# The k'v products of a head pair as two 64-column halves of the array, in a kernel of linear attention, a cosine feed-forward layer and a soft mixture of experts

## The chip, the cores and the metric

The kernel runs on one core of a Trainium2 chip. The metric is the device time of one execution in microseconds; the time before is the median of three runs. One execution was also taken by the hardware profiler, and all rows shown here are from that one.

## What is computed

All inputs are fp32. First, linear attention over 8 batches of 8 heads with 576 tokens of 64 values; then a feed-forward layer on the 4608 tokens; then a soft mixture of 8 experts with 4 slots each.

```python
kv = np.einsum('bhsd,bhse->bhde', k, v)
out = np.einsum('bhsd,bhde->bhse', q, kv)
rms = np.sqrt(np.mean(out * out, axis=-1, keepdims=True) + 1e-06)
x = (out / rms * g_norm)            # laid out as 4608 x 512
h = x @ w_in                        # 512 -> 2048
x = (h * np.cos(h)) @ w_out         # 2048 -> 512
logits = x @ phi                    # 32 slots
```

The mixture takes a softmax over the tokens of each slot, two expert layers with relu, and a softmax over the slots of each token. The change touches the first line alone: for each batch and head, `kv` is a 64x64 matrix, summed over 576 tokens.

## The kernel before, in words

The tokens are worked on in 12 blocks of 384 (`NB`, index `j`). Of each two batches, two blocks hold the first 384 tokens of one batch each, and the third holds the last 192 of both (`spans`). Each block runs 16 steps (`f`), one per 128 columns of `w_in`. A step is `main` (line 368; its 12 products are at line 375), then the cosine on ScalarE and VectorE (`fr_tt`, `round_off`, `cos_b`, `cos_c`, lines 386 to 416), with other work of PE put between the main products: transposes of the attention output (`att_xT`, line 233), logits (lines 458 and 467), the slot sums (`slot_acc`, line 533), the attention outputs (`att_out`, line 201) and the k'v products (`kv_pair`, lines 178 to 190).

The order is fixed by hand. `PLAN["start"]` lists the tokens of the start one by one, `PLAN["one"]` and `PLAN["two"]` the order within a step of the first two blocks, and the other entries of `PLAN` say in which step of which block each piece of side work runs. The four pairs of batch 0 are the tokens `kv.1 kv.2 kv.0 kv.3` of the start; those of batch 1 stand in the first step, those of batches 2 and 3 in blocks 1 to 3 (`PLAN["K"]`), and those of batch b from 4 on at steps 14, 17, 18 and 19 of a block (`PLAN["kv"]`). PE carries its instructions out in this order; the other engines and SP, which issues all the loads, have orders of their own that follow from the same lists.

`load_kv` (line 161) loads k and v of one batch and one pair of heads: 128 tokens in the partitions, four groups of them, 128 columns for the two heads of the pair. There are four such buffers. The remaining 64 tokens of two batches share one tile (`load_rem`, line 166); `kz` holds k of these with the other batch's 64 rows at zero.

`kv_pair` makes one 128x128 product per group, k as weights and v moving, all five summed in one PSUM tile: four at line 182, the one of the remainder at line 184. Its diagonal 64x64 blocks are k'v of the two heads; the other two blocks would be k of one head with v of the other and are not read. The two copies (`copy_on`, line 140: on ScalarE for batch 0, on VectorE for all others) put the diagonal blocks into `kvbd`, a 128x128 tile per pair with zeros elsewhere, from which `att_out` makes the attention output of both heads at once. `at_bank` (line 136) hands out the four PSUM banks that this side work shares; `main` has three of its own.

In `att_out`, a block of one batch takes 128 tokens as weights; the third block of each two batches takes 64 tokens of each batch as weights, and writes the two products into partitions 0 to 63 and 64 to 127 of the result.

A row gives a product's form as rows x columns of the weights: `128*128` uses all the array, `128*64` one half of its columns, `128*32` a quarter, `64*128` one half of its rows. Behind it stands the size of the moving operand.

Of the kernel before, what the change touches and what calls it, by code (L numbers as in the profile page):

```python
# [40 lines left out]
    stop=None,  # L41
    start=(
# [4 lines left out]
    ),  # L47
# [28 lines left out]
def tile_linear_attention__ffn_cos__soft_moe(  # L76
# [14 lines left out]
    nc = tc.nc  # L91
# [44 lines left out]
    def at_bank(name):  # L136
        return ps_a.tile([128, 512], F32, tag="at", name=name)

    def copy_on(e, out, in_):
        (nc.vector.tensor_copy if e else nc.scalar.copy)(out=out, in_=in_)  # L140


    q_t, kv_t, vr_t = {}, {}, {}
    kz = rem_p.tile([128, 2, 512], F32, tag="kr", name="kz")
# [31 lines left out]


    def kv_pair(b, pr):
        ps = at_bank("kvps")[:, 0:128]
        t = kv_t.pop((b, pr))  # L180
        for r in range(4):
            nc.tensor.matmul(out=ps, lhsT=t[:, 0, r, :], rhs=t[:, 1, r, :], start=(r == 0), stop=False)  # L182
        cc = slice(pr * 128, pr * 128 + 128)
        nc.tensor.matmul(out=ps, lhsT=kz[:, b % 2, cc], rhs=vr_t[b // 2][:, cc], start=False, stop=True)  # L184
        t = kvbd[b % 2]
        e = PLAN["ke"][b] if b < 2 else 2
        copy_on(e, t[0:64, pr, 0:64], ps[0:64, 0:64])
        copy_on(e, t[64:128, pr, 64:128], ps[64:128, 64:128])

        kv_done.add((b, pr))  # L190

# [642 lines left out]
    for b in range(1, B):  # L834
        p, i = divmod(b, 2)
        n, sl = 3 * p - 2 + i, PLAN["kv"]
        if b < 4:
            n, sl = PLAN["K"][b - 1]
        for pr in range(4):
            at2(n, sl[pr], kv_pair, b, pr)  # L840
# [96 lines left out]
    def token(t, f):  # L937
        k, *arg = t.split(".")
        if k.upper() in steps:
            out = int(k.islower())  # L940
            w = int(arg[0]) if arg else f + (PLAN["LO"] if out else PLAN["LI"])
            if w < NF and (arg or w >= (PLAN["PO"] if out else PLAN["PI"])):
                ck(k.upper(), w, out)
                steps[k.upper()](w, out)
        elif arg:
            a = int(arg[0])
            dict(kv=lambda: kv_pair(0, a), ao=lambda: att_out(0, a), xs=lambda: att_xs(0, a),
                 xT=lambda: att_xT(0, a), lo=lambda: att_lo(0, a), warm=lambda: warm(a),
                 win=lambda: load_win(a), wout=lambda: load_wout(a), lkv=lambda: load_kv(a // 4, a % 4),
                 rem=lambda: load_rem(a) if a == 0 else load_kz(0, 1), q=lambda: load_q(a))[k]()  # L950
        else:
            j = int(k[1])
            f -= L * j
            if 0 <= f < NF:
                dict(m=main, s=lambda j, f: run(side, j, f), f=fr_tt, r=round_off, p=lambda j, f: run(post, j, f),
                     b=cos_b, c=cos_c, e=lambda j, f: run(fin, j, f), l=lambda j, f: run(loads, j, f))[k[0]](j, f)
# [103 lines left out]
```

## Time and profile before

| what | us |
|---|---|
| median of 3 runs | 719.67 |
| lowest and highest run | 717.18, 719.83 |
| the profiled execution: its own time | 720.89 |
| its span, from first to last instruction | 719.0 |
| TensorE (PE) busy in the span | 689.0 |
| TensorE loading weights (PEld) | 574.3 |
| VectorE (DVE) busy | 527.1 |
| ScalarE (ACT) busy | 443.8 |
| GpSimd (POOL) busy | 106.5 |

The time of an execution is a little longer than the span of its instructions. Weight loads run beside the products, so the shares of PE and PEld aren't added. A product's busy time contains its way through the array, which overlaps with the next product; what a product costs in a stream is the distance between starts, not its duration. A core's granted clock of TensorE is given as a share of its full speed, 1.00 at most.

### The profile page before, as it was taken

The numbers are of one execution on the slowest core, as the hardware profiler recorded it, in microseconds if no ns is written. First come the engines' busy times: TensorE is split into PE (matmuls) and PEld (weight loads), VectorE is DVE, ScalarE is ACT, GpSimd is POOL, SyncE is SP. The second block draws the span as 40 slices with busy tenths as digits, with TensorE's granted clock in tenths as the row PEclk, the third lists the DMA queues.
The fourth block names the chain that finished last, engine by engine and source line by source line (L and its number), as shares of the span: only waits on it lengthen the run. The fifth ranks groups of instructions, "written<-read, shape, count | busy, mean of one in ns | idle before, by whom it ended". The sixth has DMA issues, their size and how long they took to land.

```text
span 719.0 us, 13016 instructions
## 1 busy us (share of the span) xinstructions
PE 689.0 (96%) x4780; PEld 574.3 (80%) x4780; DVE 527.1 (73%) x1101; ACT 443.8 (62%) x929; POOL 106.5 (15%) x104
## 2 busy tenths in 40 slices
PE   7879999999999999999999999999999999999984
PEld 7768998886998987998898879889979797864353
DVE  2998998477888878788888887888887874345144
ACT  2567997675666676575576756656757557551143
POOL 2342333100302111112012011110120210000400
PEclk9998999999999999999999999999999999999997
DMA  9953452022742674564525745735249278989997
GB/s 323 377 190 138 176 188 78 4 80 100 210 122 67 183 206 124 169 179 103 147 77 148 205 146 154 213 84 152 73 117 305 51 242 269 348 321 347 356 370 320
DMA packets 73886, 134.09 MB, mean 186 GB/s; under 512 B 8416, under 2 KB 50016, under 8 KB 73056
## 3 DMA queue, kind: packets, MB, share of 16 engines
q1 hardware_dynamic: 73824, 133.27, 58.7%
q8 instruction: 38, 0.62, 0.3%
q14 instruction: 24, 0.20, 0.1%
HBM read 91.29 MB, written 13.63 MB: 146 GB/s over the span
## 4 chain that ended last, share of the span: by engine, by line
PE 82%; DVE 9%; ACT 4%; issue 2%; DMA 1%; SPq 0%; POOL 0%; DVEq 0%; ACTq 0%
PE h L375 50%; PE ab L533 5%; PE kvps L182 4%; PE l L458 4%; PE ops L201 4%; PE xTps L233 2%; PE tr L431 2%; PE eo L689 2%; PE eh L663 2%; DVE gT L410 1%; DVE tt L396 1%; PE l L467 1%; PE fo L714 1%; PE kvps L184 1%; DVE tr L416 1%
## 5 line engine op out<-in xcount | busy, mean ns | idle before, releaser
L375 PE MATMUL h<-xt,w 128*128 128x384 f32 x2304 | 438.0, 342 | 1.6 <-DVE xt L246 1.2
L375 PEld LDWEIGHTS h<-xt,w 128*128 128x128 f32 x2304 | 397.2, 189 | 29.1 <-DVE gT L410 8.9
L401 ACT ACTIVATE fr<-tt 128x384 f32<-128x384 f32 x192 | 100.4, 524 | 136.5 <-DVE tt L396 136.0
L410 DVE TENSOR_TENSOR gT<-fr,h 128x384 f32<-128x384 f32 x186 | 102.8, 553 | 58.6 <-ACT fr L401 58.4
L213 POOL TENSOR_TENSOR ri<-ss,mhalf 128x8 f32<-128x8 f32 x36 | 65.5, 1825 | 430.8 <-DVE ss L211 430.8
L396 DVE SCALAR_TENSOR_TENSOR tt<-tt,fr 128x384 f32<-128x384 f32 x192 | 106.5, 559 | 28.9 <-ACT tt L391 27.5
L391 ACT ACTIVATE tt<-fr 128x384 f32<-128x384 f32 x192 | 100.9, 525 | 6.1
L389 ACT ACTIVATE fr<-h 128x384 f32<-128x384 f32 x192 | 92.7, 483 | 18.2 <-PE h L375 18.0
L416 DVE STREAM_TRANSPOSE tr<-gT 128x384 f32<-128x384 f32 x144 | 83.3, 579 | 5.1 <-DVE gT L410 0.2
L237 ACT ACTIVATE xt<-xTps,gn 128x512 fp32r<-128x512 f32 x36 | 24.6, 686 | 27.8 <-PE xTps L233 27.4
L182 PEld LDWEIGHTS kvps<-kv 128*128 128x128 f32 x256 | 31.8, 191 | 9.9 <-issue 6.4
L201 PE MATMUL ops<-kvA,q 128*64 128x128 f32 (+1 forms) x384 | 38.2, 278 | 1.3 <-ACT g L140 1.3
L201 PEld LDWEIGHTS ops<-kvA,q 128*64 128x64 f32 (+1 forms) x384 | 33.9, 164 | 5.2 <-issue 2.8
L182 PE MATMUL kvps<-kv 128*128 128x128 f32 x256 | 35.2, 280 | 1.8 <-DMA kv<-in_kv 1.7
L246 DVE SCALAR_TENSOR_TENSOR xt<-xTps,gn,xt 128x512 fp32r<-128x512 f32 x36 | 26.4, 738 | 12.8 <-ACT xt L237 12.5
L313 POOL TENSOR_TENSOR w<-st_m,w 128x512 fp32r<-128x512 f32 x16 | 26.7, 1670 | 54.3 <-ACT w L308 41.1
L533 PE MATMUL ab<-g,d 128*32 128x512 f32 x288 | 33.5, 596 | 0.3 <-DVE d L522 0.3
L458 PE MATMUL l<-gT,wp 128*32 128x384 f32 x312 | 33.3, 498 | 0.0
L140 ACT COPY g<-tr 128x384 f32<-128x384 f32 (+1 forms) x64 | 23.4, 393 | 7.7 <-PE tr L431 7.4
L210 DVE TENSOR_REDUCE ss<-sq 128x8 f32<-128x512 f32 x33 | 22.2, 672 | 5.0 <-ACT sq L208 4.8
L208 ACT ACTIVATE sq<-ops 128x512 f32<-128x512 f32 x33 | 19.6, 593 | 9.1 <-PE ops L201 9.1
L222 DVE TENSOR_TENSOR xs<-ops,ri 128x512 f32<-128x512 f32 x33 | 22.3, 682 | 2.4 <-POOL ri L213 2.4
(133 smaller groups left out, 631.3 us busy)
## 6 DMA issues: line engine op xcount, KB each, us to landing
g<-tr SPq DMA_DIRECT2D x288, 96.0 KB
kv<-in_kv SPq DMA_DIRECT2D x32, 512.0 KB
ew<-in_w SPq DMA_DIRECT2D x26, 512.0 KB
ew<-in_w SPq DMA_DIRECT2D x43, 256.0 KB
out<-ot SPq DMA_DIRECT2D x12, 768.0 KB
q<-in_qT SPq DMA_DIRECT2D x11, 768.0 KB
rw<-in_w_in SPq DMA_DIRECT2D x16, 512.0 KB
st_b<-in_w_outT SPq DMA_DIRECT2D x16, 512.0 KB
```

The costliest lines, as they stand in the source:

```text
L182: nc.tensor.matmul(out=ps, lhsT=t[:, 0, r, :], rhs=t[:, 1, r, :], start=(r == 0), stop=False)
L201: nc.tensor.matmul(out=ps[p0:p0 + n, pr * 128:(pr + 1) * 128], lhsT=q_t[j][:, pr, c0:c0 + n], rhs=kvbd[b % 2][:, pr, :], start=True, stop= ...
L213: nc.gpsimd.tensor_tensor(out=ri[:, :, 0], in0=ss, in1=mhalf, op=ALU.pow)
L375: nc.tensor.matmul(out=ps, lhsT=w[:, a, kk, :], rhs=x[:, b, kk, :], start=(n == 0), stop=(n == 3 * KD - 1))
L389: nc.scalar.activation(out=fr, in_=ps, func=AF.Copy, bias=0.25, scale=INV_2PI)
L391: nc.scalar.activation(out=tt, in_=fr, func=AF.Copy, bias=ROUND_M)
L396: nc.vector.scalar_tensor_tensor(out=tt, in0=tt, scalar=-ROUND_M, in1=fr, op0=ALU.add, op1=ALU.subtract)
L401: nc.scalar.activation(out=fr, in_=tt, func=AF.Sin, scale=-TWO_PI_DOWN)
L410: nc.vector.tensor_tensor(out=g, in0=fr, in1=h_t.pop((j, f)), op=ALU.mult)
L416: nc.vector.transpose(out=tr_t[j, h][:, :, o, :], in_=g.rearrange("p (b t) -> p b t", t=32))
L458: nc.tensor.matmul(out=l_t[j][32 * o:32 * o + 32, :], lhsT=wp[:, f, :], rhs=gT_t.pop((j, f)), start=(c == 0), stop=(c == (2 if j == NB - 1 ...
L533: nc.tensor.matmul(out=ps[32 * c:32 * c + 32, :], lhsT=d[:, t, :], rhs=gs[c // 2][t][:, (c % 2) * 512:(c % 2) * 512 + 512], start=(t == 0) ...
```

## The change

Each 128-column product of `kv_pair` becomes two products of 64 columns, one per head, written to partitions 0 to 63 and 64 to 127 of the same PSUM tile. Each has 64 columns of k as weights and 64 columns of v moving, and all 128 rows. The PSUM tile has 64 columns instead of 128, and the second copy reads its columns 0 to 63. The blocks that nobody reads are no longer made. Nothing else is changed: no load, no order, no buffer.

```diff
     def kv_pair(b, pr):
-        ps = at_bank("kvps")[:, 0:128]
+        ps = at_bank("kvps")[:, 0:64]
         t = kv_t.pop((b, pr))
+        hh = [slice(0, 64), slice(64, 128)]
         for r in range(4):
-            nc.tensor.matmul(out=ps, lhsT=t[:, 0, r, :], rhs=t[:, 1, r, :], start=(r == 0), stop=False)
-        cc = slice(pr * 128, pr * 128 + 128)
-        nc.tensor.matmul(out=ps, lhsT=kz[:, b % 2, cc], rhs=vr_t[b // 2][:, cc], start=False, stop=True)
+            for h in hh:
+                nc.tensor.matmul(out=ps[h], lhsT=t[:, 0, r, h], rhs=t[:, 1, r, h], start=(r == 0), stop=False)
+        for h in hh:
+            cc = slice(pr * 128 + h.start, pr * 128 + h.stop)
+            nc.tensor.matmul(out=ps[h], lhsT=kz[:, b % 2, cc], rhs=vr_t[b // 2][:, cc], start=False, stop=True)
         t = kvbd[b % 2]
         e = PLAN["ke"][b] if b < 2 else 2
         copy_on(e, t[0:64, pr, 0:64], ps[0:64, 0:64])
-        copy_on(e, t[64:128, pr, 64:128], ps[64:128, 64:128])
+        copy_on(e, t[64:128, pr, 64:128], ps[64:128, 0:64])
```

## Rows read from the trace of the kernel before

**Rows 1.** The page: busy time by engine, and the chain that ended last.

```profile
PE 689.0 (96%) x4780; PEld 574.3 (80%) x4780; DVE 527.1 (73%) x1101; ACT 443.8 (62%) x929; POOL 106.5 (15%) x104
...
PE 82%; DVE 9%; ACT 4%; issue 2%; DMA 1%; SPq 0%; POOL 0%; DVEq 0%; ACTq 0%
PE h L375 50%; PE ab L533 5%; PE kvps L182 4%; PE l L458 4%; PE ops L201 4%; PE xTps L233 2%; PE tr L431 2%; PE eo L689 2%; PE eh L663 2%; DVE gT L410 1%; DVE tt L396 1%; PE l L467 1%; PE fo L714 1%; PE kvps L184 1%; DVE tr L416 1%
```

**Rows 2.** Stages: us, busy PE, PEld, DVE, ACT, POOL, clock, DMA share, GB/s.

```profile
8.00:12.00 4.00, 4.00 (x38) 4.00 (x37) 0.00 (x0) 2.52 (x7) 0.00 (x0) 1.00 1.13 334
...
29.00:34.00 5.00, 4.94 (x47) 4.58 (x47) 4.63 (x14) 3.65 (x6) 1.14 (x1) 1.00 1.01 386
...
50.00:56.00 6.00, 3.39 (x24) 2.51 (x22) 6.00 (x10) 3.03 (x7) 2.40 (x2) 0.72 0.77 262
...
190.00:216.00 26.00, 26.00 (x171) 23.98 (x170) 22.96 (x55) 17.04 (x36) 5.22 (x10) 1.00 0.53 157
...
290.00:312.00 22.00, 22.00 (x147) 19.98 (x146) 18.16 (x44) 13.34 (x27) 0.19 (x1) 1.00 0.61 178
```

**Rows 3.** Tile kvps: records, duration in ns (least/median/most), first and last start.

```profile
L182 PE MATMUL kvps<-kv x256: 272/275/377, 7.7 to 506.3; 128*128 128x128 f32 x128
...
L184 PE MATMUL kvps<-vr,kz x64: 275/275/275, 8.7 to 506.6; 128*128 128x128 f32 x64
L140 DVE COPY kvA<-kvps x56: 177/222/230, 32.4 to 507.1; 64x64 f32<-64x64 f32 x56
```

**Rows 4.** Timeline of PE, two pairs in a row: start, us from start to end.

```profile
201.09 1.05 PE L182 MATMUL kvps<-kv 128*128 128x128 f32 x8
201.98 0.39 PE L184 MATMUL kvps<-vr,kz 128*128 128x128 f32 x2
202.20 1.06 PE L182 MATMUL kvps<-kv 128*128 128x128 f32 x8
```

**Rows 5.** Timeline of PE, a pair right behind logits of 32 columns.

```profile
305.72 1.16 PE L182 MATMUL kvps<-kv 128*128 128x128 f32 x8
306.71 0.39 PE L184 MATMUL kvps<-vr,kz 128*128 128x128 f32 x2
```

**Rows 6.** Timeline of PE, transposes to logits, with attention output in halves, then whole.

```profile
284.90 0.60 PE L233 MATMUL xTps<-ident,xs 128*128 128x128 f32 x4
285.43 1.09 PE L201 MATMUL ops<-kvA,q 128*64 128x128 f32 x16
...
292.92 0.85 PE L458 MATMUL l<-gT,wp 128*32 128x384 f32 x8
...
334.99 0.60 PE L233 MATMUL xTps<-ident,xs 128*128 128x128 f32 x4
335.42 1.06 PE L201 MATMUL ops<-kvA,q 128*128 128x128 f32 x8
...
342.66 0.85 PE L458 MATMUL l<-gT,wp 128*32 128x384 f32 x8
```

**Rows 7.** Stretches of line 201 alone, output in halves; x: products, loads under way.

```profile
261.79:261.84 0.05, 0.04 (x2) 0.04 (x2) 1.00 0.86 167
261.84:261.95 0.11, 0.11 (x2) 0.11 (x4) 1.00 1.14 249
261.95:261.97 0.02, 0.02 (x4) 0.02 (x4) 1.00 0.96 205
261.97:262.06 0.09, 0.09 (x4) 0.09 (x4) 1.00 0.87 193
262.06:262.08 0.02, 0.02 (x6) 0.02 (x4) 1.00 1.00 162
```

**Rows 8.** Timeline of the start: PE and ScalarE at the first pairs.

```profile
7.70 1.16 PE L182 MATMUL kvps<-kv 128*128 128x128 f32 x8 [1.72 <-DMA kv<-in_kv]
...
9.16 1.28 ACT L140 ACT_TABLE_LOAD   x1 [9.16 <-PE kvps L184]
...
12.27 2.95 PE L201 MATMUL ops<-kvA,q 128*128 128x128 f32 x24
```

## The prediction

> **What bounds the kernel now.** I read the page first. TensorE (PE) is busy for 689.0 of 719.0 us, VectorE for 527.1, and the chain that ended last is 82% PE work; line 182, the k'v products, stands in it with 4% and line 184, their remainder, with 1% [rows 1]. Then the table by stage. From 62 us on PE has no idle time in the stages that hold k'v pairs, while VectorE has 3 to 4 us to spare; two of them stand for the others: PE 26.00 of 26.00 us and VectorE 22.96 in 190:216, 22.00 of 22.00 and 18.16 in 290:312 [rows 2]. The first 60 us are different: DMA runs at a share of 1.13 in 8:12, and in 50:56 VectorE is busy for 6.00 of 6.00 us while PE waits for 2.6 of them [rows 2]. So a microsecond of PE time saved after 62 us is a microsecond of the kernel; one saved before it may not be.
>
> Next, the pairs themselves. The program has 32 of them, with four products of line 182 and one of line 184 each; the trace has 256 and 64 records, so each fp32 product is two passes over the array, ten passes a pair [rows 3]. Two pairs stand back to back at 201.09 and 202.20: 1.11 us a pair, 0.111 a pass [rows 4]. Of each 128x128 result only the two 64x64 diagonal blocks are copied out; the rest is thrown away.
>
> **The change, part by part.** (a) *The stream.* Each pass of 128 weight columns and 128 moving columns becomes two passes, one per column half, with 64 of each. A pair then has 20 passes in 10 slots, if the two halves run at the same time. No row shows 64 moving columns in a 64-column tile. The nearest is the attention output of the third block of each two batches, which puts two 64-token products side by side in the array with 128 moving columns. There two products begin at once, at the start of the first stretch; 0.16 us later two more begin together (two running until 261.95, four from there), and the next two 0.11 us after these (six from 262.06) [rows 7]. So the halves do run side by side, a slot takes 0.11 us, and the first one 0.05 us more, which is its weight load of 64 columns, paid once for both halves: loaded one after the other they would have cost twice that. A slot with half the moving columns and a load of 0.05 that hides under the product before it is half as long: 0.055. I take 0.058, for the few nanoseconds of a handover that need not halve. Bounds: 0.054 (half of 0.109) below; above, 0.11, if something other than columns sets the slot. The value is nearer the lower one, because product and load of that slot both go by columns. The stream saves 10 x (0.111 - 0.058) = 0.53 us a pair.
>
> Here a rule speaks against the change. In the row, from the second slot on, the four loads are under way while two products run, and the slot stays 0.11 us, not 0.16 [rows 7]: loads hide under products of the same tiles. The Trainium skill (TensorE: Matmul & The Clock Gate, Part 3, what overlaps and what doesn't) says that a weight load overlaps running products only where the row group differs, and column halves share all their rows. By that rule a slot here would be load plus product, 0.05 + 0.055, and the change would lose; the trace disagrees for these tiles, and the sum goes by the trace.
>
> (b) *Entering and leaving the halves.* The trace has the same step in both forms: four transposes, one attention output, 36 main products, then the logits. With full-width output it takes 342.66 - 334.99 = 7.67 us, with halves 292.92 - 284.90 = 8.02 [rows 6]: 0.35 us more for the same eight slots. The start shows where: from the transposes to the output it is 0.43 us in one and 0.53 in the other, so 0.10 of draining before, plus 0.05 for the uncovered first load; the remaining 0.20 is draining and an uncovered 128-column load behind. The 13 late pairs with full-width work on both sides pay 0.35 for each of 12 insertions (two stand together at 201.09). The other 11 late pairs follow work that already sits in a narrow tile (logits, 64-row products) and pay for the entry today: the eight passes of line 182 take 306.71 - 305.72 = 0.99 us there [rows 5] against 201.98 - 201.09 = 0.89 [rows 4]. They exchange 0.10 for 0.05 at the entry and pay 0.20 at the exit: 0.15 more.
>
> Sum of the 24 late pairs: 13 x 0.53 - 12 x 0.35 = 2.69, and 11 x (0.53 - 0.15) = 4.18: **6.9 us saved**, all on PE in stages where PE never idles [rows 2].
>
> (c) *The eight early pairs.* Four run from 7.70, when their data lands, to 12.27, where the first attention output starts [rows 8]. PE alone could save 4 x 0.53 less 0.2 at the exit, 1.9 us. But the loads of the later pairs and of q come in at a saturated DMA, and ScalarE needs a 1.28 us table load before its first copy out [rows 8]; after that POOL and VectorE carry the chain. I take 0.5, between 0 and 1.9. Four more run in 29:34, where VectorE is busy for 4.63 of 5.00 us [rows 2] and copies them out in its own order; I take 0: VectorE's chain covers them, and if it didn't, another 2 us could come. Against it: longer PE waits can let the clock fall. In 50:56, after waits, the granted clock is 0.72 [rows 2], between its two levels (1.2 and 2.4 GHz). Six more microseconds like these would cost 6 x 0.28 = 1.7 us. So the start is worth +0.5, from -1.7 to +3.9, with nearly all of it below +2.
>
> (d) *The copies out* (0.22 us each on VectorE, 64x64 before and after [rows 3]) keep their size, count and order; only their source columns change. That VectorE is to do them earlier costs nothing while it has its 3 to 4 us of slack by stage; without it, the 1.1 us that a 22 us stage is to save (2 x 0.18 + 2 x 0.38) would wait for VectorE. No DMA, wait or buffer is added. The kv loads that wait on SP for a pair to be read are released a little sooner, which moves nothing that is late.
>
> Total: 6.9 + 0.5 = 7.4 us. The profiled execution took 720.89 us around its span of 719.0, so it would become 713.5; it lies 1.2 us above the median of the runs, 719.67. By the median: **712.3 us**.
>
> **The rivals.** (1) *Loads not hidden, slower.* At 64 moving columns a product may be too short to cover the next load, or the halves may be loaded in turn; a slot is then 0.05 + 0.055 = 0.107 us, hardly below today's 0.111, and the draining is paid on top. Late pairs: 13 x 0.04 - 12 x 0.35 = -3.7 and 11 x (0.04 - 0.15) = -1.2; with 0.3 at the start, 5.2 us lost: 724.9. It decides from a slot of 0.111 - (12 x 0.35 + 11 x 0.15) / 240 = 0.087 us upwards. Against it speaks that the load was hidden and shared in the nearest tile; for it, that load and product are now equally long, so nothing is left over. (This is also where the rule quoted under (a) leads.) Chance 0.11.
> (2) *PE is not fed fast enough.* A slot holds two loads and two products; at 0.058 us that is one instruction per 15 ns. The densest slot of before needs one per 27 ns [rows 7]. If 20 ns were the limit, a slot would be 0.080, the late pairs would save 240 x 0.031 - 5.85 = 1.6 us, and the time be 718.1, no change. In its favour: no row shows the rate. Against: both products of a slot begin within 0.02 us of each other [rows 7], and the main products ahead of most pairs leave time to queue instructions up. Chance 0.08.
> (3) *The gain is hidden.* VectorE, at 83 to 88% in these stages, can't follow where k'v steps shrink, and PE waits for a free PSUM bank instead; a third to a half of the saving survives: about 717. Against it: VectorE's slack per stage is three times the saving. Chance 0.08.
> My forecast keeps 0.73.
>
> **How the numbers follow.** The forecast's own ends: a slot of 0.054 and the start at +1.9 give 719.67 - 6.9 - 0.96 - 1.9 = 709.9; a clock that falls at the start gives 714.5. The range runs from 709.5 to 718.1, so that it takes in (2) and (3) and leaves out (1) and a little at each end. A measurement of this kernel can tell about 0.5%, 3.6 us, from no change. Faster by more than that: the forecast, 0.73. Within: (2), (3) and the mild end of (1): 0.18. Slower: the rest of (1), 0.09.
>
> **What the profile would show.** Right: 640 records where there were 320, ten slots of two products in each pair, some 0.058 us apart; the two pairs that stand at 201.09 and 202.20 half a microsecond apart instead of 1.11; PE still without idle time in the late stages, each like 290:312 shorter by 1.1 us; the start shorter by a microsecond at most. Wrong: slots of 0.08 or more with loads standing in the gaps (1, 2); halves of equal speed but main products waiting for VectorE (3); a granted clock below 1.00 in stages after 62 us, which no term here prices.

## The result, and the profile after

The changed kernel takes **712.23 us** (median of 4 runs, 711.48 to 712.74); the kernel before took 719.09 in the same comparison (717.18 to 719.83). The ratio is 0.990, with a 95% interval of 0.9885 to 0.9916. The profiled execution took 712.48 us around its span of 710.7, against 720.89 around 719.0.

The page of the changed kernel, the same lines as in [rows 1]:

```profile
PE 679.7 (96%) x5100; PEld 559.6 (79%) x5100; DVE 524.6 (74%) x1101; ACT 443.0 (62%) x929; POOL 106.5 (15%) x104
...
PE 81%; DVE 8%; ACT 5%; DMA 3%; issue 1%; SPq 0%; DVEq 0%; ACTq 0%
PE h L378 51%; PE ab L536 5%; PE l L461 4%; PE ops L204 4%; PE xTps L236 2%; PE kvps L184 2%; PE tr L434 2%; PE eo L692 2%; PE eh L666 2%; DVE gT L413 1%; DVE tt L399 1%; DMA rw<-in_w_in 1%; PE l L470 1%; ACT fr L404 1%; PE fo L717 1%
```

PE is busy for 9.3 us less and has 320 records more. The k'v products (now lines 184 and 187) fall from 4% and 1% of the chain to 2% for line 184; line 187 is no longer in the list. A load of `w_in` stands in the chain that wasn't there before; it belongs to the start, below.

The records of the tile `kvps`, as in [rows 3]:

```profile
L184 PE MATMUL kvps<-kv x512: 222/222/271, 7.7 to 497.9; 128*64 128x64 f32 x171
...
L187 PE MATMUL kvps<-vr,kz x128: 222/222/222, 8.2 to 498.1; 128*64 128x64 f32 x128
```

There are 640 records, which the prediction calls passes, where 320 were. PE's timeline at the two pairs that stand in a row, as in [rows 4]:

```profile
198.78 0.69 PE L184 MATMUL kvps<-kv 128*64 128x64 f32 x16
199.29 0.29 PE L187 MATMUL kvps<-vr,kz 128*64 128x64 f32 x4
199.41 0.64 PE L184 MATMUL kvps<-kv 128*64 128x64 f32 x16
199.88 0.29 PE L187 MATMUL kvps<-vr,kz 128*64 128x64 f32 x4
200.09 1.14 PE L378 MATMUL h<-xt,w 128*128 128x384 f32 x5
```

From one pair to the next it is 199.41 - 198.78 = 0.63 us; the first of the two holds the 0.05 us of its uncovered load, so a pair in the stream takes 0.58 instead of 1.11. How this comes about is seen in short stretches of line 184 alone, at the pair that begins at 297.95 (columns as in [rows 7]):

```profile
298.00:298.05 0.05, 0.05 (x2) 0.05 (x4) 1.00 0.20 20
...
298.05:298.10 0.05, 0.05 (x4) 0.05 (x6) 1.00 0.11 20
298.10:298.16 0.06, 0.06 (x6) 0.06 (x6) 1.00 0.41 34
298.16:298.22 0.06, 0.06 (x8) 0.06 (x6) 1.00 0.26 34
```

Every 0.05 to 0.06 us two more products are under way (a product is counted for its whole way through the array, so they add up), always with loads beside them. Ten slots of 0.058 us make the 0.58.

A pair right behind logits, as in [rows 5]:

```profile
301.75 0.69 PE L184 MATMUL kvps<-kv 128*64 128x64 f32 x16
302.26 0.29 PE L187 MATMUL kvps<-vr,kz 128*64 128x64 f32 x4
302.48 2.35 PE L378 MATMUL h<-xt,w 128*128 128x384 f32 x12
```

And the two late stages of [rows 2], each between the same two pieces of work as before:

```profile
187.78:212.67 24.89, 24.89 (x211) 21.89 (x211) 21.94 (x52) 16.08 (x33) 5.23 (x10) 1.00 0.55 161
286.68:307.42 20.74, 20.74 (x187) 17.93 (x186) 17.31 (x43) 13.13 (x27) 0.19 (x1) 1.00 0.61 181
```

They are 24.89 instead of 26.00 us and 20.74 instead of 22.00, and PE still never idles in them. VectorE's share stays at 88% and 83%: it doesn't become the bound.

### The profile page after: what moved, and what is told of

The parts are those of the page before. It is cut to its first block, busy times and chain, and to the rows that moved or that the text cites. A ratio compares the mean times of both kernels' runs of the same rounds, so it can differ in the third digit from the quotient of the medians.

```text
span 710.7 us, 13641 instructions
## 1 busy us (share of the span) xinstructions
PE 679.7 (96%) x5100; PEld 559.6 (79%) x5100; DVE 524.6 (74%) x1101; ACT 443.0 (62%) x929; POOL 106.5 (15%) x104
## 4 chain that ended last, share of the span: by engine, by line
PE 81%; DVE 8%; ACT 5%; DMA 3%; issue 1%; SPq 0%; DVEq 0%; ACTq 0%
PE h L378 51%; PE ab L536 5%; PE l L461 4%; PE ops L204 4%; PE xTps L236 2%; PE kvps L184 2%; PE tr L434 2%; PE eo L692 2%; PE eh L666 2%; DVE gT L413 1%; DVE tt L399 1%; DMA rw<-in_w_in 1%; PE l L470 1%; ACT fr L404 1%; PE fo L717 1%
## 5 line engine op out<-in xcount | busy, mean ns | idle before, releaser
L249 DVE SCALAR_TENSOR_TENSOR xt<-xTps,gn,xt 128x512 fp32r<-128x512 f32 x36 | 26.4, 738 | 12.1 <-ACT xt L240 11.9
L184 PEld LDWEIGHTS kvps<-kv 128*64 128x64 f32 x512 | 17.6, 137 | 14.7 <-issue 8.0
L184 PE MATMUL kvps<-kv 128*64 128x64 f32 x512 | 21.5, 227 | 3.2 <-DVE kvA L140 1.7
```

The source lines that it names most:

```text
L184: nc.tensor.matmul(out=ps[h], lhsT=t[:, 0, r, h], rhs=t[:, 1, r, h], start=(r == 0), stop=False)
```

## The experiments

All times are medians of the kernel and of the kernel before in the same comparison. As the start turned out to vary by some microseconds from run to run, the table also gives, from PE's timeline of each profiled execution, the start of the first main product of block 2 and of block 11, and the time between: that stretch holds all late pairs but one and nothing of the start. The profile is of one execution of each kernel. In kernels whose late pairs are the same it repeats to 0.01 us (442.18 and 442.17, 434.85 twice).

| kernel | us | before, us | ratio (95%) | block 2 | block 11 | between |
|---|---|---|---|---|---|---|
| before | | | | 146.38 | 588.56 | 442.18 |
| the change | 712.23 | 719.09 | 0.990 (0.9885 to 0.9916) | 145.31 | 580.16 | 434.85 |
| late pairs alone | 711.87 | 719.62 | 0.990 (0.988 to 0.9928) | 147.82 | 582.67 | 434.85 |
| early pairs alone | 719.52 | 719.62 | 1.000 (0.9986 to 1.0023) | 141.92 | 584.09 | 442.17 |
| one head after the other | 721.35 | 719.62 | 1.003 (1.0012 to 1.005) | 147.02 | 591.01 | 443.99 |
| 128 moving columns | 727.62 | 719.62 | 1.011 (1.0085 to 1.0137) | 146.79 | 593.53 | 446.74 |
| two by two | 711.62 | 719.59 | 0.988 (0.9859 to 0.9896) | 146.58 | 580.99 | 434.41 |
| also batch 3 | 710.31 | 719.59 | 0.987 (0.9845 to 0.9885) | 141.76 | 576.78 | 435.02 |
| blocks of two | 713.42, one run | 719.59 | | 145.03 | 581.08 | 436.05 |
| one pair moved | 708.96 | 718.81 | 0.986 (0.9837 to 0.9892) | 143.88 | 577.36 | 433.48 |
| two at step 19 | 709.27 | 718.81 | 0.986 (0.9838 to 0.9883) | 142.00 | 575.00 | 433.01 |

**Late pairs alone, early pairs alone.** Both forms of the function stand in the kernel, and the batch decides (the second run has `b < 2`):

```diff
+    def kv_pair(b, pr):
+        (kv_halves if b >= 2 else kv_whole)(b, pr)
```

> Batches 2 to 7 in halves, batches 0 and 1 whole as before. My theory: the gain is TensorE time of the 24 late pairs, 6.9 us by the sum (the sums of the two traces, from the last instruction ahead of a pair to the second behind it, say 7.2), so this gives about 712 to 713 us, and each late pair 0.58 us between its first and last start. Rival: the shift of the start feeds the rest (a different clock or DMA phase), and the late pairs are partly hidden behind VectorE; then this stays at 715 to 719 us.

> Batches 0 and 1 in halves, batches 2 to 7 whole as before. My theory: 0 to 1 us less than before (about 718.5), because the start is paced by DMA and VectorE; the first attention output comes about 0.8 us earlier, and what follows waits for the loads of w_in as in the changed kernel. Rival: the start holds a good part of the gain; then 714 to 717 us.

With the late pairs alone the kernel is as fast as with all, 7.75 us below before; with the early ones alone it isn't faster at all (by the interval at most 1.0 us faster or 1.7 slower). The gain is that of the late pairs; the start adds nothing that can be measured. What happens there is seen in the timeline of the changed kernel:

```profile
10.55 0.69 PE L184 MATMUL kvps<-kv 128*64 128x64 f32 x16 [0.69 <-DMA kv<-in_kv]
...
11.43 2.92 PE L204 MATMUL ops<-kvA,q 128*128 128x128 f32 x24
...
17.17 0.66 ACT L290 ACTIVATE st_m<-rw 128x512 f32<-128x512 f32 x1 [2.19 <-DMA rw<-in_w_in]
...
33.02 0.69 PE L184 MATMUL kvps<-kv 128*64 128x64 f32 x16 [1.67 <-DVE kvA L140]
```

The fourth pair now waits for its load, the first attention output comes 0.84 us earlier than in [rows 8], and ScalarE then waits 2.19 us for a load of `w_in`. In 29:34 the fourth pair of batch 1 waits 1.67 us for VectorE's copies. What PE saves, it spends waiting. How late that load lands differs between the profiled executions: the kernel before had it at 15.79 without a wait, the one with the early pairs alone at 15.69 after a wait of 0.86.

**One head after the other.** Same products, other order:

```diff
-        for r in range(4):
-            for h in hh:
+        for h in hh:
+            for r in range(4):
                 nc.tensor.matmul(out=ps[h], ...)
-        for h in hh:
             cc = ...
```

> All pairs in halves, but the five products of head 0 are all issued before those of head 1, same products and same sum. My theory: TensorE starts products in order, a half alone fills only its own columns, so a pair needs 20 slots of 0.058 us instead of 10: 1.16 us of stream and the draining on top, about 726 us (7 slower than before). Rival: the gain comes from leaving out the two blocks that nobody reads, or the array runs the halves at once in whatever order they come; then about 712 us, like the change.

It comes out between the two expectations: 9.1 us above the change from block 2 to block 11 (443.99 - 434.85). PE's timeline at one pair:

```profile
302.67 0.73 PE L184 MATMUL kvps<-kv 128*64 128x64 f32 x10
303.19 0.22 PE L186 MATMUL kvps<-vr,kz 128*64 128x64 f32 x1
303.24 0.22 PE L184 MATMUL kvps<-kv 128*64 128x64 f32 x1
303.25 0.22 PE L186 MATMUL kvps<-vr,kz 128*64 128x64 f32 x1
303.30 0.46 PE L184 MATMUL kvps<-kv 128*64 128x64 f32 x5
303.59 0.28 PE L186 MATMUL kvps<-vr,kz 128*64 128x64 f32 x2
303.80 1.51 PE L377 MATMUL h<-xt,w 128*128 128x384 f32 x7
```

Line 186 is the remainder, the last product of each head. Its two passes for head 0 (303.19, 303.25) stand between passes of head 1: the second half has begun before the first one is through. The last two passes begin at 303.59 and a slot later, 0.98 us behind the first. Less 0.05 for the first load that is sixteen times 0.058: a pair takes 17 slots, neither 10 nor 20. So both halves do have to run at the same time for the change to gain, and leaving out the unread blocks alone gains nothing, as these are left out here too; but PE's order isn't as strict as I expected.

**128 moving columns.** Halves of the weights, the whole of v moving:

```diff
-        ps = at_bank("kvps")[:, 0:64]
+        ps = at_bank("kvps")[:, 0:128]
-                nc.tensor.matmul(..., rhs=t[:, 1, r, h], ...)
+                nc.tensor.matmul(..., rhs=t[:, 1, r, :], ...)
```

(and the same at the remainder; the second copy reads columns 64 to 127 again)

> All pairs in halves of 64 weight columns, but each with all 128 columns of v moving, so the blocks that nobody reads are made again. My theory: the slot goes by the moving columns, 0.109 us as in the attention output in halves; 24 x 10 x 0.051 = 12.2 us more than the change, about 725 us, slower than before. Rival: the slot is set by the weight load of 64 columns or by the issue of four instructions; then it stays at 0.058 us and the time at 712.

```profile
303.51 1.09 PE L184 MATMUL kvps<-kv 128*64 128x128 f32 x16
304.44 0.39 PE L187 MATMUL kvps<-vr,kz 128*64 128x128 f32 x4
304.75 0.98 PE L378 MATMUL h<-xt,w 128*128 128x384 f32 x4
```

The sixteen passes of line 184 take 304.44 - 303.51 = 0.93 us, 0.05 of it the first load: eight slots of 0.11 us. From block 2 to block 11 the kernel needs 446.74 us, 11.9 more than the change (12.2 were worked out for one pair more) and 4.6 more than before. The slot goes by the moving columns, and the halves as such cost time: this kernel has the change's drains with hardly any of its gain.

**Two by two, and batch 3 as well.** What is left to save is entering and leaving:

```diff
-    kv=(14, 17, 18, 19),
+    kv=(14, 14, 18, 18),
```

(the second run has `(14, 14, 18, 18)` for batch 3 in `PLAN["K"]` too)

> The change, and the pairs of batches 4 to 7 two by two, both couples right behind logits (steps 14, 14, 18, 18 instead of 14, 17, 18, 19). My theory: what is left of the cost is entering and leaving the halves, 0.35 us for each of the two insertions per batch that fall away, so 4 x 0.70 = 2.8 us less than the change: about 709.3 us, with two pairs 0.58 us apart. Rival: two pairs at once wait for a PSUM bank that VectorE has not emptied, and TensorE idles for it; then 711 to 713 us.

> As the one before, and the pairs of batch 3 moved from steps 12, 15, 15, 19 to 14, 14, 18, 18 of their block. My theory: three insertions between full-width work (1.06 us) are exchanged for 0.15 us at each of two entries behind logits, 0.76 us less again: about 708.5 us. Rival: loads or PSUM banks of these pairs come late; then no less than the one before.

Only 0.4 us of 2.8 came between the blocks (434.41 against 434.85), and batch 3 gave back 0.6 (435.02), though the median of that run is lower. The timeline of the two-by-two run, in the step behind the place where step 19's pair had been:

```profile
307.63 1.28 ACT L508 ACT_TABLE_LOAD   x1
...
309.73 2.33 PE L378 MATMUL h<-xt,w 128*128 128x384 f32 x12
309.88 1.28 ACT L404 ACT_TABLE_LOAD   x1
...
311.17 0.53 ACT L404 ACTIVATE fr<-tt 128x384 f32<-128x384 f32 x1
...
311.73 0.55 DVE L413 TENSOR_TENSOR gT<-fr,h 128x384 f32<-128x384 f32 x1 [0.92 <-ACT fr L404]
...
312.34 0.97 PE L378 MATMUL h<-xt,w 128*128 128x384 f32 x4 [0.28 <-DVE gT L413]
```

In this step the slot softmax takes ScalarE through two table loads of 1.28 us; the cosine waits behind them, then VectorE's product, and that one frees the bank that `main` wants next. PE gets there early and stops. From one step's first main product to the next step's, the three steps from 306.54 on take 0.19, 0.44 and 0.12 us longer than in the change, and those of the other three batches the same to 0.01. Neither theory had it so: it was a bank, but of `main`, not of the k'v products, and the pair at step 19 had been the work that covered it. In the run with batch 3 as well, PE waits at the same place of that batch's block:

```profile
212.90 2.36 PE L378 MATMUL h<-xt,w 128*128 128x384 f32 x12 [0.44 <-DVE gT L413]
```

There the three steps take 0.19, 0.61 and 0.11 us longer than in the two-by-two run.

**One pair moved, two at step 19.** So the pair at 19 stays, and the one at 17 moves:

```diff
-    kv=(14, 17, 18, 19),
+    kv=(14, 14, 18, 19),
```

(the second run has `(14, 14, 19, 19)`)

> The change, with one pair of batches 4 to 7 moved: from step 17 to 14, steps 14, 14, 18, 19. My theory after the two-by-two run: an insertion between full-width work costs 0.36 us, and the pair at step 19 must stay where it is, because it covers the wait for VectorE in the step after it (0.56 us there in the two-by-two run). So four insertions fall away without a new wait: 4 x 0.36 = 1.4 us less than the change from block 2 on (565.4 us there, to about 564.0), and about 710.7 us in all, as far as the spread of the start allows. Rival: VectorE limits every step here, and any pair taken out opens a wait; then the 565.4 us stay.

> The change, with the pairs of batches 4 to 7 at steps 14, 14, 19, 19. My theory: the pairs at step 17 and 18 lose their insertions (0.36 and 0.15 us), and two pairs at step 19 cover VectorE's wait behind them better than one; 4 x 0.5 = 2.0 us less than the change from block 2 on (565.4 to 563.4), about 710.1 us. Rival: the copies of two pairs stand in VectorE's way just where it is late, and the wait moves; then 565 us or more.

(The 565.4 us of these expectations run from block 2 to the end of the span of the changed kernel, 710.7 - 145.31.) Between the blocks one pair moved gives 1.37 us (434.85 - 433.48) where 1.4 was expected, and two at step 19 give 1.84 where 2.0 was: no new wait in either. To the end of the span it is 563.9 us for the first (707.8 - 143.88), as worked out, and 564.3 for the second. What is missing there went behind block 11: 131.3 us from its start to the end of the span, against 130.5 in the change and 130.4 in the first. The reason isn't shown: the granted clock of the last 66 us was 0.90 in the second and 0.94 in the changed kernel, but 0.90 in the first as well, which lost nothing. In time both lie below the change and the kernel before: 708.96 and 709.27 us, 1.4% below the latter. Between these two nothing is decided, and of the 3 us by which they lie under the change only the 1.4 and 1.8 between the blocks are shown to be theirs.

**Blocks of two.** How far does PE look ahead? Two products of head 0, two of head 1, and so on:

```diff
-        for r in range(4):
+        for r2 in (0, 2):
             for h in hh:
-                nc.tensor.matmul(...)
+                for r in (r2, r2 + 1):
+                    nc.tensor.matmul(...)
```

> The change with another order of the same products: two products of head 0, then two of head 1, then again, then the two remainders. From the run with one head after the other I take that TensorE begins a product of the other half early only if at most three passes are ahead of it in its order; then a pair takes 11 slots instead of 10, 0.64 us from first to last start instead of 0.58. Rival: there is no such limit in this order, or the early starts of that run came from the end of an accumulation group; then 0.58 us, or 14 slots and more (0.8 us).

```profile
298.03 0.73 PE L185 MATMUL kvps<-kv 128*64 128x64 f32 x16
298.54 0.33 PE L188 MATMUL kvps<-vr,kz 128*64 128x64 f32 x4
298.81 0.98 PE L379 MATMUL h<-xt,w 128*128 128x384 f32 x4
```

From the pair's first start to the main products behind it it is 0.78 us here; in the change it is 302.48 - 301.75 = 0.73 at the pair behind logits, and the same elsewhere. That and the 1.2 us between the blocks (436.05 - 434.85) come to 0.05 us more for each of the 23 pairs, close to the one slot (0.058) that was expected. A look ahead of about three passes fits both orders, but two orders don't prove the number, and 0.05 us is also what an uncovered load of 64 columns cost above: these times don't tell the two apart.

## Why the prediction was right

712.3 us was forecast and 712.23 measured; by the steps it is closer in some than in others. That the two agree to a tenth is partly luck: the forecast took 7.4 us from a median of 719.67, the comparison gave 6.9 below one of 719.09.

- *Step (a), the slot.* Taken as 0.058 us between bounds of 0.054 and 0.11, measured as 0.058. That the moving columns set it was an inference from one row with twice the columns; the run with 128 moving columns shows it. Rivals 1 and 2 fall with the slot of 0.058: loads are hidden, and one instruction per 15 ns is issued. The rule that I set against it (the Trainium skill, TensorE: Matmul & The Clock Gate, Part 3) doesn't hold for these halves: loads run beside the products in every stretch of line 184 shown above, and with the load uncovered the slot would have been about 0.105 us, by the estimate of rival 1 (0.05 + 0.055, which the prediction puts at 0.107; nothing hangs on the difference).
- *Step (b), entering and leaving.* The 0.35 and 0.15 us were a little high. PE's timeline has three landmarks around a pair behind logits and a pair between full-width work; before:

```profile
304.94 0.85 PE L458 MATMUL l<-gT,wp 128*32 128x384 f32 x8
...
309.05 0.81 PE L483 MATMUL lr<-ls,rep 128*128 128x384 f32 x2
...
312.92 0.27 PE L201 MATMUL ops<-kvA,q 128*128 128x128 f32 x1
```

and after:

```profile
300.97 0.85 PE L461 MATMUL l<-gT,wp 128*32 128x384 f32 x8
...
304.67 0.81 PE L486 MATMUL lr<-ls,rep 128*128 128x384 f32 x2
...
308.33 0.94 PE L204 MATMUL ops<-kvA,q 128*128 128x128 f32 x7
```

  From the first to the second, with the pair behind logits, 4.11 us became 3.70: 0.41 saved, forecast 0.53 - 0.15 = 0.38. From the second to the third 3.87 became 3.66: 0.21 saved, forecast 0.53 - 0.35 = 0.18. So the two prices are 0.12 and 0.32. Two pairs of each kind make 1.24 of the 1.26 us that the stage 290:312 lost; 1.1 was forecast. The pair that was moved away shows the price of an insertion by itself, 1.37 / 4 = 0.34.
- *The sum of the late pairs* was 6.9 us for 24, or 6.7 without the one ahead of block 2; from block 2 to block 11 442.18 - 434.85 = 7.3 went. The difference is the 0.03 us a pair of (b). Taken step by step (from one step's first main product to the next step's), the gain lies where the sum puts it: the 22 steps that hold these 23 pairs lose 7.38 us together (0.41 to 0.43 with a pair behind narrow work, 0.20 or 0.21 with one between full-width work, 0.74 with the two in a row), and no other step between the two blocks changes by more than 0.04. So nothing of the late pairs' gain is hidden, and nothing comes from elsewhere.
- *Step (c), the start*, was given 0.5 us and is nothing that can be measured (early pairs alone: 1.000). The covers named there were the right ones (loads, VectorE's copies). The cost of a falling clock that was feared there doesn't show in sum: up to block 2 the granted clock is 0.97 in the profile before and 0.96 in the one after. The half microsecond that was too much made up for what (b) left out, so the total fits better than its terms.
- *Rival 3, a hidden gain,* is wrong for this change and right one step further: with two pairs per batch taken from their old places, 0.4 instead of 2.8 us came, because VectorE and ScalarE became the bound of one step. That VectorE had 3 us to spare in a stage of 22 said nothing of that step; an average over a stage wouldn't have shown it.

## What to carry to other kernels

Where only the diagonal blocks of a product are wanted, products side by side in column halves take half the stream, if the two halves alternate closely in the order of issue and the moving operand is halved along with the weights; halving the weights alone cost 1.1%. Set against it a third of a microsecond (in this kernel) for each visit to the halves between full-width work, less where the work ahead already sits in narrow tiles, so put several visits together. Before moving such work, look for the step in which it is the cover for another engine, as a stage's average hides it.

## What had not been expected

PE begins products of the other half ahead of earlier ones: with all ten passes of head 0 issued first, head 1's passes started while head 0 had some three left, and a pair took about 17 slots, not 20 (721.35 us instead of the expected 726). So the order of the program is the order of issue, but not strictly that in which products of different halves start.

And the first 146 us of this kernel are far less steady than what follows: block 2 begins between 141.8 and 147.8 us in these profiles, in no order that the edits would explain, while the stretch up to block 11 repeats to 0.01 us when its code is the same. It goes along with TensorE's granted clock. In the three profiles that reach block 2 by 142.0 us (early pairs alone, also batch 3, two at step 19) the clock is 1.00 (2.4 GHz) throughout 29:62; in the eight others it is between 0.67 and 0.95 in 56:62. The stretch 56:62 of the kernel before and of two at step 19 (columns as in [rows 2]):

```profile
56.00:62.00 6.00, 6.00 (x28) 5.97 (x27) 4.32 (x7) 2.84 (x5) 0.18 (x1) 0.71 0.49 178
...
56.00:62.00 6.00, 6.00 (x44) 5.30 (x43) 4.86 (x8) 4.50 (x12) 1.29 (x1) 1.00 0.41 156
```

PE is busy all the time in both. Just ahead, in 50:56, it was busy for 3.39 of 6.00 us in the first [rows 2] and for 4.83 in the second. Whether the lower clock makes the start late or the longer waits of a late start lower the clock, no run here separates. Differences of a microsecond or two are therefore better read between landmarks behind the start than in the total.
